# Inverse row sums of an attention repeated by a product with ones from PSUM instead of a copy

## The chip, the cores and the metric

The kernel runs on one core of one Trainium2 chip. The metric is the device time of one execution in microseconds, as the median of three timed runs. Engines are called by the profile's names: PE is TensorE's matrix unit (PEld its weight loads), DVE is VectorE, ACT ScalarE, POOL GpSimd, SP the engine that issues the DMAs.

## What is computed

Rotary attention over 2 batches, 8 heads, 576 positions and head size 64, followed by two feed-forward blocks of 512 to 2048 to 512, the first with ELU, the second with Mish:

```python
q_rot, k_rot = rotate(q), rotate(k)
scores = scale * np.matmul(q_rot, k_rot.transpose(0, 1, 3, 2))
attn = np.exp(scores - np.max(scores, axis=-1, keepdims=True))
attn = attn / (np.sum(attn, axis=-1, keepdims=True) + 1e-09)
x = np.matmul(attn, v)                     # then heads side by side: 1152 x 512
x = elu(x @ w_in) @ w_out
x = mish(x @ w2_in) @ w2_out
```

Queries, keys, values and the output are fp32, the four weights float64. Weights and activations are split into a high and a low part so that the products keep fp32's accuracy.

## The kernel before

Two heads make a pair; there are 8 pairs. The 2 x 576 query rows of a pair are cut into nine tiles of 128 rows: four full tiles of each head, and a ninth that holds the last 64 rows of both. Attention runs in windows of two tiles. The order of every engine's instructions is written out by hand in the loop over the windows, and each engine works through its own queue in that order.

In a window the names are these. `do_S` (L425, PE) makes the scores of two tiles in two PSUM tiles `ps_s`. `do_max` (L434, DVE) takes the minimum of each score row (the queries carry a minus sign), `mn`; `do_exp` (L447, ACT) writes the exponentials `P` and their row sums `sm`. In the next window `do_T` (L494, PE) transposes `P` into the PSUM tile `psT`, and `do_evac` moves `psT` into `pt`: the first tile's on DVE (L510), the second's on ACT (L512). There is one `psT`, so PE's transposes of the second tile wait for L510. `do_av` (L518, PE) adds up the product of the values `v_t` with `pt` in the PSUM tile `psA[g]`, where g is 0 for the pair's first four tiles (256 columns) and 1 for the other five (320 columns). [...]

The sums stand one to a query row, but in `psA` the queries are columns. So the inverse sums are turned around, once for each pair and g, 16 times in all. `do_eps` (L457, ACT) gathers the sums in `rc`; `repeat_inverse` (DVE) inverts them (L461) and repeats each over 64 columns into the SBUF tile `R`: 256 columns for the four full tiles (L463), and for g = 1 another 128 for the ninth tile (L469). `do_R` (L479, PE) transposes `R` into `psA[g]`, `take_R` (L484, L486, ACT) copies that back into `R`, and after the value product `do_x` (L534, DVE) multiplies `psA[g]` by it. `do_xh` (L538, ACT) and `do_xl` (L542, DVE) split the result into `XH` and `XL`.

POOL rotates queries and keys of the next pair (L293, L295, L297) and splits them (L328, L329); it also begins and ends the weights' conversion (L96, L128), whose middle steps L100, L104 and L108 are on DVE. The weights come as float64 words and are converted on the chip. After attention, `g1_mm` (L207) and `g2_first` or `g2_second` (L752, L781) are the feed-forward products on PE. `keep_warm` (L563) fills PE's first idle time with products of zeros into `psA[1]`, columns 0 to 128.

Of the kernel before, what the change touches and what calls it, by code (L numbers as in the profile page):

```python
# [14 lines left out]
ALU = mybir.AluOpType  # L15
# [7 lines left out]
def plain(ap):  # L23
    return ap.bitcast(F32)
# [3 lines left out]
def kernel(  # L28
# [11 lines left out]
    nc = tc.nc  # L40
# [213 lines left out]
    def attention(att, ps, tail):  # L254
# [2 lines left out]
        psT = ps.tile([128, 2, 512], F32, name="psT")  # L257
        psA = [ps.tile([128, 512], F32, name=f"psA{g}") for g in range(2)]
        HEAD = [(2, slice(0, HS)), (0, slice(0, 128)), (2, slice(HS, S)), (0, slice(128, HS)), (0, slice(HS, S))]
        WARM = 20  # L260
        FIRST = {(0, 0): 6, (0, 1): 2}
        FILL = (4, 5, 0)
# [6 lines left out]
        def load_pair(p):  # L269
            t = att.tile([128, 4, S], F32, tag="qk", name="qk_t", bufs=2)  # L270
            if p == 0:
                for i, cs in HEAD:
                    if i == 2:
# [25 lines left out]
        def rope_half(p, i, eng, cs=slice(0, S)):  # L299
            for k in range(3):  # L300
                rope_part(p, i, k, eng, cs)

        def split_alloc(p):
            d = {}
            for nm in ("kh", "kl") if p < MASKED else ("kh", "kl", "ql"):
                d[nm] = att.tile([128, S], F32R, tag=nm, name=nm, bufs=2)
            for nm in ("qa",) if p < MASKED else ("ka", "qa"):
                d[nm] = att.tile([128, 2, S], F32R, tag=nm, name=nm, bufs=2)
            if p >= MASKED:
                d["qh"] = att.tile([128, S], F32R, tag="qh", name="qh", bufs=1)  # L310
            i = p % 2
            d["qb"] = qb[i]
            d["bh"], d["bl"] = bd[i]
            sp_t[p] = d
            if p < MASKED:

                eng = nc.gpsimd if p else nc.vector
                for nm in ("qa", "qb"):
                    for h in range(2):
                        eng.memset(plain(d[nm][64 - 64 * h:128 - 64 * h, h, :]), 0.0)  # L320
# [13 lines left out]
        def first_hi(i, cs, heads=(0, 1)):  # L334
            x = qk_t[0][:, i, cs]
            if i:
                nc.scalar.activation(out=sp_t[0]["kh"][:, cs], in_=x, func=AF.Copy)
            for h in () if i else heads:
                nc.scalar.activation(
                    out=own(sp_t[0]["qa"], h, cs), in_=x[64 * h:64 * h + 64], func=AF.Copy, scale=QSCALE,  # L340
                )

        def first_lo(i, cs, heads=(0, 1)):
            d = sp_t[0]
            x = qk_t[0][:, i, cs]
            if i:
                nc.vector.tensor_tensor(out=d["kl"][:, cs], in0=x, in1=plain(d["kh"][:, cs]), op=ALU.subtract)
            for h in () if i else heads:
                nc.vector.scalar_tensor_tensor(
                    out=own(d["qb"], h, cs), in0=x[64 * h:64 * h + 64], scalar=QSCALE,  # L350
                    in1=plain(own(d["qa"], h, cs)), op0=ALU.mult, op1=ALU.subtract,
                )
# [22 lines left out]
        def stack_q(p):  # L375
            d = sp_t[p]
            if p >= MASKED:
                for r in range(2):
                    spread(d["qa"], d["qh"], r)
                spread(d["qb"], d["ql"], 0)  # L380
            for r in range(2):
                sl = slice(64 * r, 64 * r + 64)
                ec = slice(S - 64, S)
                hi, lo = (own(d[nm], r, ec) for nm in ("qa", "qb")) if p < MASKED else (d["qh"][sl, ec], d["ql"][sl, ec])
                nc.sync.dma_start(out=plain(d["bh"][sl, 64 * r:64 * r + 64]), in_=plain(hi))
                nc.sync.dma_start(out=plain(d["bl"][sl, 64 * r:64 * r + 64]), in_=plain(lo))
# [72 lines left out]
        def repeat_inverse(p, g):  # L459
            r = rc_t.pop((p, g))[:, :4 + g]  # L460
            nc.vector.reciprocal(out=r, in_=r)  # L461
            B = R_t[p, g] = att.tile([128, (256, 384)[g]], F32, tag=f"R{g}", name=f"R{g}", bufs=1)
            nc.vector.tensor_scalar(  # L463
                out=B[:, 0:256].rearrange("p (t h r) -> p t h r", t=2, h=2),
                in0=r[:, 0:4].rearrange("p (h t) -> p t h", h=2).unsqueeze(3).to_broadcast([128, 2, 2, 64]),
                scalar1=1.0, scalar2=0.0, op0=ALU.mult, op1=ALU.add,
            )
            if g:
                nc.vector.tensor_scalar(  # L469
                    out=B[:, 256:384], in0=r[:, 4:5].to_broadcast([128, 128]),  # L470
                    scalar1=1.0, scalar2=0.0, op0=ALU.mult, op1=ALU.add,
                )

        def do_R(p, g):
# [75 lines left out]
        for i in range(2):  # L550
            pair = []
            for nm in ("bh", "bl"):
                t = att.tile([128, 128], F32R, name=f"{nm}{i}")
# [2 lines left out]
            bd.append(pair)  # L556
        qb = [att.tile([128, 2, S], F32R, name=f"qb{i}") for i in range(2)]
        nc.vector.memset(psT[:, 1, 0:128], 0.0)
        split_alloc(0)
        split_alloc(1)  # L560
        def keep_warm(n):
            for _ in range(n):
                nc.tensor.matmul(psA[1][:, 0:128], lhsT=zero, rhs=zero, start=True, stop=True)  # L563

        zero = plain(bd[1][1])
        keep_warm(WARM)
        for i, cs in HEAD:
            rope_half(0, i, nc.vector if i else nc.gpsimd, cs)
            if cs.stop < S or i:
                first_hi(i, cs, (0,))  # L570
        for i, cs in HEAD[:-1]:
            first_lo(i, cs, (0,))
# [44 lines left out]
        for w in range(max(av_at) + 2):  # L617
# [3 lines left out]
            for u in (a, b):  # L621
                p, i = divmod(u, TPP)
# [10 lines left out]
            if R is not None:  # L633
                repeat_inverse(*R)
# [30 lines left out]
            if w == 0:  # L665
                first_hi(*HEAD[-1])
            elif w == 1:
                first_lo(*HEAD[-1])
                stack_q(0)
# [223 lines left out]
    with tc.tile_pool(name="att", bufs=1, reuse_waits="tile") as att, tc.tile_pool(  # L893
        name="ps_att", bufs=1, space=bass.MemoryType.PSUM, reuse_waits="tile"
    ) as ps:
        with tc.manual_schedule():
            attention(att, ps, tail)
# [56 lines left out]
```

## Time and profile before

| | us |
|---|---|
| timed runs: median (lowest to highest of 3) | 587.66 (587.22 to 588.53) |
| the profiled execution's own time | 589.5 |
| its span, first to last instruction | 587.7 |
| PE busy | 558.7 (95%) |
| DVE busy | 431.3 (73%) |
| ACT busy | 363.3 (62%) |
| POOL busy | 244.5 (42%) |

Busy shares are means over stages with different limits, so the rows below are read by stage. PE's granted clock is at its upper level (0.999 of full speed) over the whole span. Times in the rows count from the start of the span. A row of the timeline gives start, duration, engine, line, operation, tiles and shapes, and in brackets how long the engine stood idle before it and what ended the wait.

### The profile page before, as it was taken

To read this page: it belongs to the slowest core of one execution; us is meant where nothing else is said; L and a number is where in the kernel's file an instruction comes from. 1 tells how busy PE (TensorE), PEld (TensorE's weight loads), DVE (VectorE), ACT (ScalarE), POOL (GpSimd) and SP (SyncE) were. 2 spreads that over 40 slices of the span, in tenths; PEclk is the share of its full clock that TensorE was granted. 3 is DMA by queue.
4 is the path that set the end of the run, shared out by engine and by line. 5 is a ranking of instruction groups with operands and counts; after the bars stand their busy time and mean duration, and the time that the engine had idled before them with its cause. 6 is when DMAs were issued, how large, how long until landed. Compare 5 with 4: busy or idle time off the path is not lost.

```text
span 587.7 us, 10232 instructions
## 1 busy us (share of the span) xinstructions
PE 558.7 (95%) x3866; PEld 504.2 (86%) x3866; DVE 431.3 (73%) x650; ACT 363.3 (62%) x646; POOL 244.5 (42%) x214
## 2 busy tenths in 40 slices
PE   7879988998998999999999999999999999999997
PEld 7756756676787999999999999998989898899985
DVE  6687998888855866777778988687578687584452
ACT  3655666666665655554455564795967867668650
POOL 6768998772021233223225442253244253341000
PEclk9999999999999999999999999999999999999999
DMA  6257677636011232222223332142052332300022
GB/s 223 86 187 237 175 212 205 203 105 163 21 53 37 73 102 78 72 95 86 73 78 127 119 108 80 65 150 84 9 151 56 108 113 67 108 19 1 19 90 89
DMA packets 43121, 60.69 MB, mean 103 GB/s; under 512 B 13760, under 2 KB 31936, under 8 KB 42304
## 3 DMA queue, kind: packets, MB, share of 16 engines
q1 hardware_dynamic: 43072, 60.05, 33.8%
q8 instruction: 30, 0.49, 0.4%
q14 instruction: 19, 0.16, 0.1%
HBM read 46.20 MB, written 2.36 MB: 83 GB/s over the span
## 4 chain that ended last, share of the span: by engine, by line
PE 40%; issue 30%; DVE 15%; POOL 11%; ACT 3%; DMA 1%; SPq 0%; POOLq 0%; DVEq 0%; ACTq 0%
PE ps_h L781 17%; PE ps_s L207 14%; DVE mn L434 5%; POOL wu L96 4%; DVE pt L510 3%; PE ps_s L425 3%; PE psT L494 3%; POOL wi1l L128 2%; POOL wo0l L128 2%; DVE R L463 2%; POOL wi0l L128 2%; POOL wo1l L128 2%; ACT P L447 1%; PE psA L518 1%; DMA qk_t<-in_qk_dram 1%
## 5 line engine op out<-in xcount | busy, mean ns | idle before, releaser
L447 ACT ACTIVATE P<-ps_s,mn 128x576 f32<-128x576 f32 x72 | 52.9, 738 | 32.3 <-DVE mn L434 31.9
L494 PE MATMUL psT<-idn,P 128*128 128x128 f32 (+1 forms) x360 | 53.0, 278 | 16.8 <-DVE pt L510 16.6
L494 PEld LDWEIGHTS psT<-idn,P 128*128 128x128 f32 (+1 forms) x360 | 38.2, 134 | 33.4 <-DVE pt L510 30.4
L434 DVE TENSOR_REDUCE mn<-ps_s 128x1 f32<-128x576 f32 x72 | 51.9, 751 | 19.6 <-PE ps_s L425 19.1
L128 POOL TENSOR_TENSOR wo0l<-wu,wo0h 128x512 fp32r<-128x512 f32 x16 | 27.3, 1708 | 89.5 <-ACT wo0h L125 89.5
L100 DVE TENSOR_SCALAR wu<-wu 128x512 int32<-128x512 int32 x64 | 32.9, 513 | 35.5 <-POOL wu L96 35.5
L207 PE MATMUL ps_s<-XH,wi0h 128*128 128x288 f32 x256 | 55.1, 297 | 1.9 <-DVE tb L242 1.9
L207 PE MATMUL ps_s<-XH,wi1h 128*128 128x288 f32 x256 | 55.0, 296 | 1.5 <-ACT tb L709 1.5
L207 PE MATMUL ps_s<-XH,wi1l 128*128 128x288 f32 x256 | 54.9, 295 | 0.0
L207 PE MATMUL ps_s<-XL,wi1h 128*128 128x288 f32 x256 | 54.8, 295 | 0.0
L207 PE MATMUL ps_s<-XL,wi0h 128*128 128x288 f32 x256 | 54.6, 295 | 0.0
L207 PE MATMUL ps_s<-XH,wi0l 128*128 128x288 f32 x256 | 54.6, 295 | 0.0
L96 POOL TENSOR_SCALAR wu<-raw 128x512 f32<-128x512 f32 x64 | 48.6, 762 | 11.1 <-DMA raw<-in_w_in_dram 6.5
L104 DVE SCALAR_TENSOR_TENSOR wu<-raw,wu 128x512 int32<-128x512 int32 x64 | 49.3, 771 | 1.9
L128 POOL TENSOR_TENSOR wi1l<-wu,wi1h 128x512 fp32r<-128x512 f32 x16 | 23.0, 1441 | 66.7 <-ACT wi1h L125 66.7
L128 POOL TENSOR_TENSOR wo1l<-wu,wo1h 128x512 fp32r<-128x512 f32 x16 | 24.5, 1531 | 61.1 <-ACT wo1h L125 61.1
L108 DVE SCALAR_TENSOR_TENSOR wu<-raw,wu 128x512 int32<-128x512 int32 x64 | 48.3, 755 | 1.6
L518 PE MATMUL psA<-pt,v_t 128*64 128x256 f32 (+1 forms) x320 | 46.5, 417 | 0.0
L238 ACT ACTIVATE tb<-ps_s 128x576 f32<-128x576 f32 x30 | 19.6, 652 | 40.5 <-PE ps_s L207 38.9
L207 PEld LDWEIGHTS ps_s<-XH,wi0h 128*128 128x128 f32 x256 | 41.4, 188 | 3.6 <-DVE tb L242 2.4
L207 PEld LDWEIGHTS ps_s<-XH,wi1h 128*128 128x128 f32 x256 | 41.7, 188 | 2.3 <-ACT tb L709 1.7
L128 POOL TENSOR_TENSOR wi0l<-wu,wi0h 128x512 fp32r<-128x512 f32 x16 | 23.0, 1442 | 47.1 <-ACT wi0h L125 47.1
(150 smaller groups left out, 1522.2 us busy)
## 6 DMA issues: line engine op xcount, KB each, us to landing
raw<-in_w_in_dram SPq DMA_DIRECT2D x32, 512.0 KB, 3.7
raw<-in_w_out_dram SPq DMA_DIRECT2D x32, 512.0 KB, 3.3
qk_t<-in_qk_dram SPq DMA_DIRECT2D x6, 1152.0 KB, 5.3
qa<-qh SPq DMA_DIRECT2D x24, 144.0 KB, 2.5
v_t<-in_vp_dram SPq DMA_DIRECT2D x8, 320.0 KB, 3.0
out_dram<-Y SPq DMA_DIRECT2D x9, 256.0 KB, 2.0
ka<-kh SPq DMA_DIRECT2D x12, 144.0 KB, 2.8
ka<-kl SPq DMA_DIRECT2D x12, 144.0 KB, 2.5
```

The costliest lines, as they stand in the source:

```text
L96: nc.gpsimd.tensor_scalar(out=u, in0=high.bitcast(F32), scalar1=REBASE, scalar2=0.0, op0=ALU.mult, op1=ALU.add)
L100: nc.vector.tensor_scalar(out=ui, in0=ui, scalar1=3, scalar2=0x7FFFFFF8, op0=ALU.logical_shift_left, op1=ALU.bitwise_and)
L104: nc.vector.scalar_tensor_tensor(out=ui, in0=high, scalar=-0x80000000, in1=ui, op0=ALU.bitwise_and, op1=ALU.bitwise_or)
L108: nc.vector.scalar_tensor_tensor(out=ui, in0=low, scalar=29, in1=ui, op0=ALU.logical_shift_right, op1=ALU.bitwise_or)
L128: nc.gpsimd.tensor_tensor(out=lo, in0=u, in1=plain(hi), op=ALU.subtract)
L207: nc.tensor.matmul(o[:, j, :HS], lhsT=w[:, cc, :], rhs=x[:, b, cc, j * HS:j * HS + HS], start=(k == 0), stop=(k == 3 * NC - 1),)
L238: nc.scalar.activation(out=v2(g), in_=h, func=AF.Relu, scale=-1.0)
L434: nc.vector.tensor_reduce(out=m, in_=psS[u][:, :, :HS], axis=AX.XY, op=ALU.min)
L447: nc.scalar.activation(out=P.rearrange("p (j n) -> p j n", j=2), in_=psS.pop(u)[:, :, :HS], func=AF.Exp, scale=-1.0, bias=mn_t.pop(u), acc ...
L494: nc.tensor.transpose(tv[:w, c, :], P[:, c * 128:c * 128 + w], idn)
L518: nc.tensor.matmul(o[64 * h:64 * h + 64, :n], lhsT=v_t[p][:, c, 64 * h:64 * h + 64], rhs=pt_t[p, g][:, h, c, :], start=(c == 0), stop=(c = ...
L781: nc.tensor.matmul(o, lhsT=l, rhs=w, start=(k == 0), stop=(k == 3 * GF - 1))
```

## The change

Both copies in `repeat_inverse` become products. The first operand is a stretch of ones in `psA[g]`, columns 384 to 512, which no product or transpose writes; the second is the inverse sums, repeated by the access pattern as before. The ones are written once, by two memsets on DVE at the start.

```diff
+        ONES = slice(384, 512)
...
             B = R_t[p, g] = att.tile([128, (256, 384)[g]], F32, tag=f"R{g}", name=f"R{g}", bufs=1)
-            nc.vector.tensor_scalar(
+
+            ones = psA[g][:, ONES]
+            nc.vector.tensor_tensor(
                 out=B[:, 0:256].rearrange("p (t h r) -> p t h r", t=2, h=2),
-                in0=r[:, 0:4].rearrange("p (h t) -> p t h", h=2).unsqueeze(3).to_broadcast([128, 2, 2, 64]),
-                scalar1=1.0, scalar2=0.0, op0=ALU.mult, op1=ALU.add,
+                in0=ones.rearrange("p (h r) -> p h r", h=2).unsqueeze(1).to_broadcast([128, 2, 2, 64]),
+                in1=r[:, 0:4].rearrange("p (h t) -> p t h", h=2).unsqueeze(3).to_broadcast([128, 2, 2, 64]),
+                op=ALU.mult,
             )
             if g:
-                nc.vector.tensor_scalar(
-                    out=B[:, 256:384], in0=r[:, 4:5].to_broadcast([128, 128]),
-                    scalar1=1.0, scalar2=0.0, op0=ALU.mult, op1=ALU.add,
+                nc.vector.tensor_tensor(
+                    out=B[:, 256:384], in0=ones, in1=r[:, 4:5].to_broadcast([128, 128]), op=ALU.mult
                 )
...
         nc.vector.memset(psT[:, 1, 0:128], 0.0)
+        for g in range(2):
+            nc.vector.memset(psA[g][:, ONES], 1.0)
```

The order of every engine stays the same. On DVE, at the first pair's g = 1, the queue held before (`mn` row minima, `rc` sums, `R` their repeated inverses, `pt` the emptied transposes):

```order
L510 COPY pt_331<-psT 128x5x128
L461 RECIPROCAL rc<-rc 128x5
L463 TENSOR_SCALAR R_436<-rc 128x256
L469 TENSOR_SCALAR R_436<-rc 128x128
L434 TENSOR_REDUCE mn<-ps_s 128x1 x2
```

and at the same place in the changed kernel, whose lines are numbered a little higher:

```order
L513 COPY pt_333<-psT 128x5x128
L462 RECIPROCAL rc<-rc 128x5
L466 TENSOR_TENSOR R_438<-psA_79,rc 128x256
L473 TENSOR_TENSOR R_438<-psA_79,rc 128x128
L435 TENSOR_REDUCE mn<-ps_s 128x1 x2
```

Only the two instructions that write `R` differ; they now read `psA` as well. The waits on semaphores are the same too.

## Rows read from the trace of the kernel before

**Rows 1.** Busy time by stretch: from:to, length, engines' busy us (instructions), clock, DMA

```profile
21.00:170.00 149.00, 132.08 (x1000) 101.21 (x999) 122.77 (x195) 96.06 (x232) 99.66 (x79) 1.00 0.56 162
170.00:588.00 418.00, 410.44 (x2760) 387.84 (x2758) 294.56 (x428) 258.48 (x396) 131.09 (x114) 1.00 0.26 79
```

**Rows 2.** Waits of PE, 35.9 to 136 us: total, times, longest

```profile
PE psT L494 <- DVE pt L510: 12.0, 13, 1.7
```

**Rows 3.** Group of line L463: count, busy us, mean ns, idle before

```profile
L463 DVE TENSOR_SCALAR R<-rc 128x256 f32<-128x256 f32 x16 | 11.6, 723 | 0.5
```

**Rows 4.** Single lines of DVE: shortest, median, longest in ns; first and last start

```profile
L463 DVE TENSOR_SCALAR R<-rc x16: 293/644/1486, 21.2 to 167.9; 128x256 f32<-128x256 f32 x16
L469 DVE TENSOR_SCALAR R<-rc x8: 214/689/697, 37.3 to 168.1; 128x128 f32<-128x128 f32 x8
L542 DVE TENSOR_TENSOR XL<-psA,XH x16: 410/450/493, 44.9 to 184.5; 128x256 fp32r<-128x256 f32 x8, 128x320 fp32r<-128x320 f32 x8
```

**Rows 5.** Timeline of POOL and DVE, 84 to 88 us

```profile
84.16 1.89 POOL L295 TENSOR_TENSOR qk_t<-qk_t,tab 128x576 f32<-128x576 f32 x1
84.69 0.41 DVE L542 TENSOR_TENSOR XL<-psA,XH 128x256 fp32r<-128x256 f32 x1
85.02 0.16 DVE L461 RECIPROCAL rc<-rc 128x4 f32<-128x4 f32 x1
85.22 0.99 DVE L463 TENSOR_SCALAR R<-rc 128x256 f32<-128x256 f32 x1
```

**Rows 6.** Timeline of the first pair's g = 1, 35.8 to 41 us

```profile
35.81 1.43 POOL L297 TENSOR_TENSOR qk_t<-qk_t 128x576 f32<-128x576 f32 x1
35.90 1.49 DVE L463 TENSOR_SCALAR R<-rc 128x256 f32<-128x256 f32 x1
37.20 0.72 POOL L328 TENSOR_SCALAR kh<-qk_t 128x576 fp32r<-128x576 f32 x1
37.28 0.43 PE L425 MATMUL ps_s<-kl,qa 128*128 128x288 f32 x2
37.31 0.70 DVE L469 TENSOR_SCALAR R<-rc 128x128 f32<-128x128 f32 x1
37.91 1.41 DVE L434 TENSOR_REDUCE mn<-ps_s 128x1 f32<-128x576 f32 x2
39.25 0.81 DVE L510 COPY pt<-psT 128x640 f32<-128x640 f32 x1
40.11 0.77 PE L494 MATMUL psT<-idn,P 128*128 128x128 f32 x5 [1.28 <-DVE pt L510]
```

**Rows 7.** Timeline of PE, 104 to 106 us

```profile
104.37 1.30 PE L518 MATMUL psA<-pt,v_t 128*64 128x320 f32 x8
```

**Rows 8.** Timeline of DVE, 151 to 154 us, where POOL is idle

```profile
151.83 0.29 DVE L463 TENSOR_SCALAR R<-rc 128x256 f32<-128x256 f32 x1
152.04 0.22 DVE L469 TENSOR_SCALAR R<-rc 128x128 f32<-128x128 f32 x1
152.49 1.42 DVE L434 TENSOR_REDUCE mn<-ps_s 128x1 f32<-128x576 f32 x2 [0.23 <-PE ps_s L425]
```

**Rows 9.** Timeline of DVE and PE, 131 to 136 us

```profile
131.53 1.39 DVE L463 TENSOR_SCALAR R<-rc 128x256 f32<-128x256 f32 x1
133.44 1.41 DVE L434 TENSOR_REDUCE mn<-ps_s 128x1 f32<-128x576 f32 x2
135.64 0.76 PE L494 MATMUL psT<-idn,P 128*128 128x128 f32 x5 [1.74 <-DVE pt L510]
```

**Rows 10.** Timeline of DVE at the start

```profile
5.17 0.46 DVE L293 TENSOR_TENSOR qk_t<-qk_t,tab 128x288 f32<-128x288 f32 x1 [0.75 <-DMA qk_t<-in_qk_dram]
```

**Rows 11.** Groups of DVE, 44 to 160 us, and line L104's shortest, median, longest

```profile
L104 DVE SCALAR_TENSOR_TENSOR wu<-raw,wu 128x512 int32<-128x512 int32 x7 | 6.6, 946 | 0.0
L108 DVE SCALAR_TENSOR_TENSOR wu<-raw,wu 128x512 int32<-128x512 int32 x6 | 6.3, 1048 | 0.0
L104 DVE SCALAR_TENSOR_TENSOR wu<-raw,wu x64: 676/693/1672, 59.3 to 526.5; 128x512 int32<-128x512 int32 x64
```

## The prediction

> **What bounds the kernel now.** I first read the busy times by stage, to find the engine that a saved microsecond must reach. From 170 us to the end TensorE works 410.44 of 418 us: the two feed-forward stages are TensorE's, and nothing that the change touches runs there except at their very start. In the attention stage, 21 to 170 us, TensorE works 132.08 of 149 us, VectorE 122.77, GpSimd 99.66 [rows 1]. So attention has 17 us in which TensorE stands still, and VectorE is the nearest to full. The view of waits then says who TensorE waits for: between 35.9 and 136 us it waited 13 times, 12.0 us in all, and each time for the VectorE line that empties psT, L510 [rows 2]. What counts is therefore whether VectorE reaches L510 earlier in those windows.
>
> Next come the instructions that the change replaces. The 16 copies of L463 take 11.6 us, 723 ns each on average [rows 3]. That mean hides two kinds: L463 runs from 293 to 1486 ns for the same 256 columns, L469 from 214 to 697 ns. The nearest thing to the new instruction, L542 (one operand in psA, one in SBUF, result in SBUF), stays between 410 ns (256 columns) and 493 ns (320) [rows 4]. Why L463 stretches is seen where both run under one GpSimd instruction. L295 on GpSimd lasts from 84.16 to 86.05. L542 starts at 84.69 inside it and takes 0.41 us, its bare time. L463 starts at 85.22 inside it and ends at 86.21, just after GpSimd ends [rows 5]. The first pair shows the same twice: L463 and L469 end at 37.39 and 38.01, after GpSimd ends at 37.24 and 37.92 [rows 6]. Where GpSimd is idle the pair takes 0.29 and 0.22 us [rows 8]. I went through all 24 copies: each long one ends 0.1 to 0.2 us after a GpSimd instruction ends, each short one has no GpSimd work beside it. So a copy from SBUF alone waits until GpSimd is through; an instruction with one operand in PSUM does not.
>
> **What the change costs and saves.** The product reads ones from psA and the sums from SBUF, writes SBUF, and is queued exactly where the copy was, behind the same single wait. A product of 256 columns should take L542's 0.41 us; 64 more columns cost L542 about 0.08 us, so 128 columns take some 0.27 us. From start to next start it is less, since VectorE's instructions overlap: L542 at 84.69 is followed after 0.33 us by the next instruction (the reciprocal). I take 0.33 us for 256 columns, and 0.20 for 128 (0.33 less twice 0.067). A product for g=0 then occupies 0.33 us of the queue, the two for g=1 0.53. The bounds for this unseen form: from below the bare copy, 0.26 and 0.21 us; from above L542's full duration with no overlap, 0.41 and 0.27. Over the ten places below (four of 256 columns, six pairs) the ends move the sum by 0.5 us up or 0.9 us down, since at 35.90 and 102.76 something else sets the gain.
>
> Ten of the sixteen places have a GpSimd instruction beside them. For each I take the gap from the start of L463 to the start of the next row-minimum L434. After the change the gap is 0.33 or 0.53, unless the scores that L434 reads come later. L434 is followed by L510, so what the gap loses L510 gains, and TensorE's following transpose L494 gains it up to the length of its wait:
> - 35.90: gap 2.01, the scores set it. The second score product ends at 37.71, the second minimum starts at 37.74, and L510 0.67 us later at 38.41 instead of 39.25. Gain 0.84, of a TensorE wait of 1.28 [rows 6].
> - 55.14: 0.95 to 0.53, gain 0.42 of 1.31. 64.08: 0.69 to 0.33, gain 0.36 of 0.50. 76.07: 1.04 to 0.53, gain 0.51 of 1.73. 85.22: 0.91 to 0.33, gain 0.58 of 1.01. 93.56: 1.91 to 0.53, gain 1.38 of 1.73.
> - 102.76: 0.79 to 0.33, but TensorE is busy with the value product until 105.67 and begins its transpose 0.08 us later [rows 7]: gain 0.05.
> - 114.02: 1.05 to 0.53, the scores hold it by another 0.12: gain 0.40 of 0.98. 123.17: 0.91 to 0.33, gain 0.58 of 1.00.
> - 131.53: 1.91 to 0.53, gain 1.38 of 1.74, the last of the ten [rows 9].
>
> The sum is 6.5 us. Every gain fits into its wait, so TensorE moves by it, and everything behind TensorE too.
>
> The other six places have bare copies, which grow by about 0.07 us (256 columns) or 0.1 us (pair). At 21.21, 45.39, 140.74 and 151.83 the minimum behind them waits for the scores anyway, at 151.83 for 0.23 us [rows 8]. At 160.17 and 167.88 TensorE is busy with other products past the point at which it needs the result. I put these at nothing; without that cover they would cost 0.5 us. The two new memsets sit at the head of VectorE's queue, among memsets of 0.17 us; behind them L293 waits 0.75 us for its load [rows 10], which covers 0.3 us. The warm-up products of TensorE wait for an earlier memset and do not move.
>
> The profiled execution took 589.5 us with a span of 587.7 us; 6.5 less is 583.0 and a span of 581.2. It lies 1.8 us above the median of the three timed runs, 587.66. The same 6.5 us off the median gives 581.2 us, 1.1% less.
>
> [...] Bare, the copy of 256 columns takes 0.29 us and an instruction with a PSUM operand 0.41 [rows 4]. [...]
>
> **Rivals.** First: the gain is taken back at the next instruction that GpSimd holds up. VectorE also makes the weights' integer passes (L100, L104, L108), all in SBUF. From 44 to 160 us the seven of L104 take 6.6 us and the six of L108 6.3, where 13 bare ones at 0.68 would take 8.8 [rows 11]: they lose 4.1 us. If such a pass comes earlier while GpSimd's instruction ends when it did, it ends when it did, and the transpose behind it too. For it: GpSimd is busy two thirds of the stage [rows 1], so a pass that comes earlier seldom finds it idle. Against: after most of these passes the next minimum waits for scores. If half of the gain goes so, 3.3 us stay: 584.4 us.
>
> Second: the passes fall better than before. How long one waits depends only on where in a GpSimd instruction it falls, from nothing (0.68 us in all) to a whole one (1.67 us, the longest L104), and shifted by 1 to 6 us they all fall anew. If four passes on the path wait some 0.5 us less each, the gain is 8.5: 579.2 us.
>
> Third, the other side: the long copies are long for a reason that the product shares, so it waits for GpSimd as well and only the rate changes. Its place is the ten gaps: ten times 0.12 and six times 0.07 more, 1.6 us: 589.3 us, slower. It decides if the product's durations spread with GpSimd's. Against it stand all 16 copies of L542, none above 493 ns.
>
> Fourth: nothing is left, because GpSimd, or the loads that follow it, sets the pace of attention once VectorE is faster: 587.7 us. Against it: from 35.9 to 136 us TensorE waited for nothing but L510 [rows 2].
>
> **How the numbers follow.** The forecast has 0.53 (580.7 to 582.1 us by the bounds of the product's cost), taken back 0.20, falls better 0.20, slower 0.04, nothing left 0.03. The time given is the forecast's, 581.2. The range goes from 578.8, a little below the second rival, to 584.6, just above the first. A measurement here tells about 0.2%, 1.2 us, from no change: forecast and the first two rivals are faster, 0.93; same 0.03; slower 0.04.
>
> **What would show it.** Right: all products of 256 columns near 0.41 us and of 128 near 0.28 whatever GpSimd does; TensorE's waits for L510 in the attention stage down from about 12 us to about 5.5; the feed-forward stages as long as before, only starting 6 to 7 us earlier. Wrong: a spread in the products' durations (third rival), unchanged gaps with longer weight passes (first), or a new wait of TensorE for a load (fourth).

## The result, and the profile after

| | before | after |
|---|---|---|
| median of 5 runs | 587.60 us (587.22 to 588.53) | 580.23 us (579.38 to 581.99) |
| ratio, 95% interval | | 0.987 [0.9855, 0.9884] |
| profiled execution | 589.5 us, span 587.7 us | 581.99 us, span 580.2 us |
| granted clock, mean | 0.999 | 0.999 |

The kernel is 7.4 us faster where 6.5 were forecast (581.2 us). The time lies half a microsecond below the forecast's own range (580.7 to 582.1 us), inside the larger one (578.8 to 584.6), and halfway between the forecast and its second rival (579.2). The lines moved: L463 is now L466, L469 is L473, L434 is L435, L510 is L513, L494 is L497.

Busy time by stretch, in the columns of [rows 1], cut where the attention stage now ends:

```profile
21.00:164.00 143.00, 132.85 (x1007) 102.02 (x1005) 115.48 (x194) 96.12 (x233) 99.60 (x80) 1.00 0.59 169
164.00:581.00 417.00, 408.95 (x2749) 386.96 (x2748) 296.06 (x428) 257.66 (x396) 127.98 (x112) 1.00 0.26 80
```

TensorE does the same work in the first stretch (132.85 us against 132.08) in 143 us instead of 149. Its idle time there has shrunk from 17 to 10 us. Feed-forward is as long as it was (417 us against 418).

The new instructions, in the columns of [rows 4]:

```profile
L466 DVE TENSOR_TENSOR R<-psA,rc x16: 424/425/425, 20.9 to 160.6; 128x256 f32<-128x256 f32 x16
L473 DVE TENSOR_TENSOR R<-psA,rc x8: 280/280/283, 36.0 to 160.9; 128x128 f32<-128x128 f32 x8
```

This is the reading that matters: the shortest and the longest of the 16 products are 1 ns apart, where the copies spread from 293 to 1486. GpSimd is as busy as before (99.60 us), so nothing about its work changed. Only VectorE's waiting for it is gone from these instructions.

TensorE's waits for the emptying of psT, from 15 to 175 us, first in the kernel before and then in the kernel after (total, times, longest):

```profile
PE psT L494 <- DVE pt L510: 16.6, 19, 1.7
```

```profile
PE psT L497 <- DVE pt L513: 9.9, 17, 1.7
```

The difference of 6.7 us is nearly the whole gain. Three places of the timeline of after, and the start of TensorE's queue:

```profile
1.95 1.44 PE L568 MATMUL psA<-bl 128*128 128x128 f32 x5 [1.95 <-DVE psA L563]
...
35.58 1.43 POOL L298 TENSOR_TENSOR qk_t<-qk_t 128x576 f32<-128x576 f32 x1
35.68 0.42 DVE L466 TENSOR_TENSOR R<-psA,rc 128x256 f32<-128x256 f32 x1
36.02 0.28 DVE L473 TENSOR_TENSOR R<-psA,rc 128x128 f32<-128x128 f32 x1
36.73 1.56 DVE L435 TENSOR_REDUCE mn<-ps_s 128x1 f32<-128x576 f32 x2 [0.43 <-PE ps_s L426]
38.20 0.82 DVE L513 COPY pt<-psT 128x640 f32<-128x640 f32 x1
39.07 0.77 PE L497 MATMUL psT<-idn,P 128*128 128x128 f32 x5 [0.45 <-DVE pt L513]
...
72.01 1.28 POOL L128 TENSOR_TENSOR wi0l<-wu,wi0h 128x512 fp32r<-128x512 f32 x1
72.03 1.80 DVE L104 SCALAR_TENSOR_TENSOR wu<-raw,wu 128x512 int32<-128x512 int32 x1
...
76.71 0.76 PE L497 MATMUL psT<-idn,P 128*128 128x128 f32 x5 [1.59 <-DVE pt L513]
...
116.07 0.72 DVE L108 SCALAR_TENSOR_TENSOR wu<-raw,wu 128x512 int32<-128x512 int32 x1
```

At the first place, both products run wholly under L298 of GpSimd (35.58 to 37.01) and are through at 36.30. The minimum then waits 0.43 us for the scores, as forecast. TensorE's wait of 1.28 us [rows 6] is now 0.45: 0.83 gained, 0.84 forecast.

### The profile page after: what moved, and what is told of

It is laid out like the page before. It is cut to its first block, busy times and chain, and to the rows that moved or that the text cites. A ratio compares the mean times of both kernels' runs of the same rounds, so it can differ in the third digit from the quotient of the medians.

```text
span 580.2 us, 10234 instructions
## 1 busy us (share of the span) xinstructions
PE 557.8 (96%) x3866; PEld 504.0 (87%) x3866; DVE 425.9 (73%) x652; ACT 362.8 (63%) x646; POOL 241.1 (42%) x214
## 4 chain that ended last, share of the span: by engine, by line
PE 45%; issue 29%; POOL 11%; DVE 10%; ACT 2%; DMA 1%; SPq 0%; POOLq 0%; DVEq 0%
PE ps_h L786 17%; PE ps_s L207 14%; PE ps_s L426 5%; PE psT L497 5%; POOL wu L96 4%; DVE mn L435 3%; PE psA L521 3%; DVE pt L513 3%; POOL wi1l L128 2%; POOL wo0l L128 2%; POOL wi0l L128 2%; POOL wo1l L128 2%; DMA qk_t<-in_qk_dram 1%; ACT P L448 1%; PE psA L482 1%
## 5 line engine op out<-in xcount | busy, mean ns | idle before, releaser
L435 DVE TENSOR_REDUCE mn<-ps_s 128x1 f32<-128x576 f32 x72 | 52.1, 753 | 19.2 <-PE ps_s L426 18.4
L497 PE MATMUL psT<-idn,P 128*128 128x128 f32 (+1 forms) x360 | 53.1, 278 | 9.9 <-DVE pt L513 9.9
L128 POOL TENSOR_TENSOR wo0l<-wu,wo0h 128x512 fp32r<-128x512 f32 x16 | 25.4, 1590 | 88.4 <-ACT wo0h L125 79.0
L497 PEld LDWEIGHTS psT<-idn,P 128*128 128x128 f32 (+1 forms) x360 | 38.2, 135 | 26.3 <-DVE pt L513 23.3
L100 DVE TENSOR_SCALAR wu<-wu 128x512 int32<-128x512 int32 x64 | 31.9, 498 | 33.4 <-POOL wu L96 33.4
L96 POOL TENSOR_SCALAR wu<-raw 128x512 f32<-128x512 f32 x64 | 48.6, 761 | 11.5 <-DMA raw<-in_w_in_dram 6.9
L104 DVE SCALAR_TENSOR_TENSOR wu<-raw,wu 128x512 int32<-128x512 int32 x64 | 49.9, 779 | 1.9
L108 DVE SCALAR_TENSOR_TENSOR wu<-raw,wu 128x512 int32<-128x512 int32 x64 | 48.2, 752 | 1.6
L207 PEld LDWEIGHTS ps_s<-XH,wi1l 128*128 128x128 f32 x256 | 41.3, 188 | 0.0
```

The costliest lines, as they stand in the source:

```text
L96: nc.gpsimd.tensor_scalar(out=u, in0=high.bitcast(F32), scalar1=REBASE, scalar2=0.0, op0=ALU.mult, op1=ALU.add)
L100: nc.vector.tensor_scalar(out=ui, in0=ui, scalar1=3, scalar2=0x7FFFFFF8, op0=ALU.logical_shift_left, op1=ALU.bitwise_and)
L104: nc.vector.scalar_tensor_tensor(out=ui, in0=high, scalar=-0x80000000, in1=ui, op0=ALU.bitwise_and, op1=ALU.bitwise_or)
L108: nc.vector.scalar_tensor_tensor(out=ui, in0=low, scalar=29, in1=ui, op0=ALU.logical_shift_right, op1=ALU.bitwise_or)
L128: nc.gpsimd.tensor_tensor(out=lo, in0=u, in1=plain(hi), op=ALU.subtract)
L207: nc.tensor.matmul(o[:, j, :HS], lhsT=w[:, cc, :], rhs=x[:, b, cc, j * HS:j * HS + HS], start=(k == 0), stop=(k == 3 * NC - 1),)
```

## The experiments

Two theories stood against each other from the start. Mine: one operand in PSUM is what lets the instruction run beside GpSimd, and the gain is what the copies lost. The rival: the gain has another source (the operation tensor_tensor instead of tensor_scalar, the memsets, or weight passes that fall anew). The second question was where the 0.9 us beyond the forecast came from.

### 1. The same product with the ones in SBUF

```diff
-            ones = psA[g][:, ONES]
+            ones = one_t
...
-        for g in range(2):
-            nc.vector.memset(psA[g][:, ONES], 1.0)
+        one_t = att.tile([128, 128], F32, name="one_t")
+        nc.vector.memset(one_t, 1.0)
```

> The product stays, but its ones lie in SBUF (128 columns, written once) and not in psA. [...] Then the products stretch again at the ten places with GpSimd beside them, to about 0.5 to 1.6 us from about 0.42 bare, and the time is 587 to 590 us, the copy's or a little more because the bare product is 0.12 us longer. [...]

Measured: 592.27 us, 1.0072 [1.0056, 1.0087] of before. Single lines:

```profile
L466 DVE TENSOR_TENSOR R<-one_t,rc x16: 425/774/1610, 20.5 to 171.1; 128x256 f32<-128x256 f32 x16
L473 DVE TENSOR_TENSOR R<-one_t,rc x8: 284/746/1494, 36.9 to 171.5; 128x128 f32<-128x128 f32 x8
```

The same operation with the same shapes spreads again, from its bare 425 ns to 1610. So it is not the operation. The rate is the product's and the waiting is the copy's, which makes this the third rival of the prediction come true: it gave 589.3 us, 587 to 590 us were expected here, and the run shows more. Part of the reason is seen in one place:

```profile
53.32 1.60 POOL L296 TENSOR_TENSOR qk_t<-qk_t,tab 128x576 f32<-128x576 f32 x1
54.32 0.89 DVE L466 TENSOR_TENSOR R<-one_t,rc 128x256 f32<-128x256 f32 x1
55.01 1.47 POOL L298 TENSOR_TENSOR qk_t<-qk_t 128x576 f32<-128x576 f32 x1
55.13 1.49 DVE L473 TENSOR_TENSOR R<-one_t,rc 128x128 f32<-128x128 f32 x1
56.55 1.41 DVE L435 TENSOR_REDUCE mn<-ps_s 128x1 f32<-128x576 f32 x2
57.88 0.81 DVE L513 COPY pt<-psT 128x640 f32<-128x640 f32 x1
58.74 1.21 PE L497 MATMUL psT<-idn,P 128*128 128x128 f32 x5 [2.05 <-DVE pt L513]
```

L466 ends at 55.21, past the end of L296 and just after L298 has started. L473 then starts inside L298 and waits it out as well. TensorE stood idle for 2.05 us, and what followed is its granted clock (the number before the last two):

```profile
58.00:60.00 2.00, 1.26 (x7) 1.22 (x8) 1.79 (x4) 0.89 (x5) 1.92 (x3) 0.73 0.54 127
60.00:62.00 2.00, 2.00 (x10) 2.00 (x9) 0.86 (x2) 1.28 (x3) 2.00 (x2) 0.50 0.73 175
62.00:64.00 2.00, 2.00 (x16) 1.38 (x16) 1.82 (x4) 1.51 (x4) 2.00 (x2) 0.92 0.89 206
```

The granted clock is down to 0.50 for some 3.4 us; two score products together take 0.66 to 0.83 us there, and 0.42 to 0.51 from 65 us on. Another such stretch follows an idle time of 1.93 us at 99 us (0.68 to 0.82 us for two). This I had not counted; the two stretches account for the 3 us beyond the rival's price, if each is worth the 1.5 us that experiment 4 finds for one. One of the four executions shows a mean granted clock of 0.997 where the other three show 0.994, and it is the shortest, 590.95 us.

A long wait did not always bring the clock down. A third one in this trace is as long as the second, and the clock behind it stays at 1.00:

```profile
138.81 0.77 PE L497 MATMUL psT<-idn,P 128*128 128x128 f32 x5 [1.93 <-DVE pt L513]
```

```profile
140.00:142.00 2.00, 2.00 (x17) 1.58 (x17) 1.53 (x3) 1.60 (x6) 0.00 (x0) 1.00 0.99 228
```

What else decides, no run here shows.

### 2. The copy kept, but reading its sums from PSUM

```diff
-            nc.vector.reciprocal(out=r, in_=r)
+            q = psA[g][:, 384:388 + g]
+            nc.vector.reciprocal(out=q, in_=r)
+            r = q
```

There are no ones and no product; the reciprocal writes five columns of psA, and the two tensor_scalar copies read them.

> The copy stays as before, but the reciprocal writes its 4 or 5 columns into psA (columns 384 on) and the copies read them there; no ones, no memsets. Theory (one operand in PSUM is enough): the copies take about 0.40 to 0.43 us for 256 columns and 0.28 for 128 whatever GpSimd does, and the time is that of the change, 580.2 us within 0.7. Rival (the operation counts, a copy waits and a product does not): spread from 0.4 to 1.5 us as before and 587 us.

Measured: 581.76 us, 0.9893 [0.9879, 0.9908]. The copies:

```profile
L465 DVE TENSOR_SCALAR R<-psA x16: 424/425/425, 20.5 to 160.3; 128x256 f32<-128x256 f32 x16
L471 DVE TENSOR_SCALAR R<-psA x8: 280/281/283, 35.5 to 160.7; 128x128 f32<-128x128 f32 x8
```

The copy with its input in PSUM has the product's durations within a nanosecond. Its time misses the expected 580.2 us within 0.7: it is 1.5 us above, though the intervals of the two ratios still overlap. The traces differ by 0.1 us only (counted from the first place on, the lead over before grows by 7.0 us here and by 7.1 in after); where the rest comes from is not shown. Together with experiment 1 this settles what frees these instructions: for copy and product alike, it is the operand in PSUM and not the operation.

It does not follow that every instruction from SBUF waits. The reciprocal just ahead reads and writes SBUF alone, and it is never held up, under L295 of GpSimd in [rows 5] for instance (0.16 us):

```profile
L461 DVE RECIPROCAL rc<-rc x16: 160/176/191, 21.0 to 167.7; 128x4 f32<-128x4 f32 x8, 128x5 f32<-128x5 f32 x8
```

Side by side: 425 ns flat with one operand in PSUM, 425 to 1610 with both operands in SBUF (experiment 1), 293 to 1486 for the tensor_scalar from SBUF [rows 4], 160 to 191 for the reciprocal from SBUF. What spares the reciprocal, whether that it is short or something else, this run does not show.

### 3. The memsets alone

```diff
         nc.vector.memset(psT[:, 1, 0:128], 0.0)
+        for g in range(2):
+            nc.vector.memset(psA[g][:, 384:512], 1.0)
```

> The copies of before, with the two memsets of the change at the head, whose ones nobody reads. Theory: the memsets lie under the wait for the first load and the warm-up products start 0.5 us later without a price, so time as before, 587.7 us within 0.5. Rival: a part of the 7.4 us comes from the later head, because the weight passes fall anew against GpSimd; then 585 us or less with the same long copies.

Measured: 587.75 us, 0.9999 [0.999, 1.0008]. The memsets cost and bring nothing. As in after, the first warm-up product starts at 1.96 us instead of 1.48, since it now waits for them.

### 4. The two halves apart

The product for g = 1 alone (256 and 128 columns), then for g = 0 alone (256 columns); the other half keeps the copy:

```diff
+            if g == 1:
+                ones = psA[g][:, ONES]
+                nc.vector.tensor_tensor(
...
+            else:
                 nc.vector.tensor_scalar(
```

> Only the places with g = 1 (the pairs of instructions) use the product, g = 0 keeps the copy. By the sum over places: 0.84 + 0.42 + 0.51 + 1.38 + 0.40 + 1.38 = 4.9 us less than before: 582.7 us. Rival (a shift of any size makes the weights' integer passes fall anew, and that moves as much as the places themselves): off from that by 1 us or more, and the two halves do not add up to 7.4 us.

> Only the places with g = 0 use the product. By the sum over places: 0.36 + 0.58 + 0.05 + 0.58 = 1.6 us less than before: 586.0 us; with the other half 6.5 us together. Rival (the integer passes fall anew): off by 1 us or more, with durations of L100, L104 and L108 that differ from before by as much.

Measured: g = 1 alone 580.96 us, 0.9883 [0.9868, 0.9898]; g = 0 alone 587.4 us, 0.9993 [0.9981, 1.0005]. The gains, 7.0 and 0.6 us, add up to 7.6, near the change's 7.4, but the split is not that of the places: 4.9 and 1.6 were expected. In the trace of g = 0 alone, most of what its own places bring is lost at one point. There a pair of copies (g = 1) starts at 74.87 and the emptying of psT behind it at 77.27; TensorE stands idle, then runs slowly, and the next emptying has lost another 0.83 us against before:

```profile
78.13 0.77 PE L508 MATMUL psT<-idn,P 128*128 128x128 f32 x5 [2.11 <-DVE pt L524]
```

```profile
76.00:78.00 2.00, 0.02 (x2) 0.00 (x0) 2.00 (x4) 1.28 (x3) 1.97 (x2) 1.00 0.80 188
78.00:80.00 2.00, 1.87 (x14) 1.87 (x15) 0.55 (x3) 1.30 (x5) 2.00 (x2) 0.89 0.99 230
80.00:82.00 2.00, 2.00 (x11) 1.60 (x11) 1.42 (x3) 1.43 (x4) 1.92 (x3) 0.50 0.72 162
82.00:84.00 2.00, 2.00 (x12) 0.77 (x10) 1.98 (x4) 0.82 (x4) 2.00 (x2) 0.76 0.09 17
```

In the trace of before the transpose at this place waited 1.73 us, and the granted clock stayed at 1.00 in the 6 us behind it. So a few tenths of a microsecond more of idle time had a second price here, if the clock is the cause.

The trace is one of ten executions of this kernel. Five show a mean clock of 0.996 or 0.997 over the span, as this one does, and took 587.56 to 589.63 us; the other five show 1.00 and took 586.42 to 587.24. Their medians are 588.17 and 586.64 us. So the drop came in half of the executions of one and the same kernel, and cost about 1.5 us where it came. Without it g = 0 alone gains 1.3 us, near the 1.6 expected; it is then the 7.0 of g = 1 that lies off.

### 5. TensorE kept at work in that wait

Six products into unused columns, ahead of the waiting transpose, in the kernel with the product for g = 0 alone:

```diff
+            if w == 14:
+                for _ in range(6):
+                    nc.tensor.matmul(psT[:, 1, 256:384], lhsT=idn, rhs=idn, start=True, stop=True)
             if 0 < w <= NW:
                 do_T(b - 2)
```

> The product for the halves with g=0 alone (587.4 us), with six extra products of TensorE into unused columns just ahead of the transpose that there waited 2.11 us, after which the granted clock was 0.50 for about 3.4 us. Theory: the stretch at the lower clock follows from that long idle time; with the six products (0.85 us) in it the transpose waits about 1.2 us, the granted clock stays at 1.00, and the step of +0.83 us at the next emptying of psT goes: 586.4 us. Rival: the step is VectorE's own, and stays with the clock at 1.00: 587.4 us.

Measured: 588.62 us, 1.0015 [1.0004, 1.0025] of before. It tests nothing: the columns are unused, but they belong to psT, so the products waited for its emptying as the transpose had.

```profile
78.04 2.61 PE L671 MATMUL psT<-idn 128*128 128x128 f32 x12 [2.09 <-DVE pt L524]
```

(The six products are recorded as twelve.) The idle time was as long, the clock fell again (0.50 from 79 to 81 us; five of the eleven executions show a mean clock of 0.997), and the products came on top. The second try puts them into `psA[1][:, 0:128]`, free at this point; nothing else differs.

> As in the first try, the product for g=0 alone with six extra products of TensorE ahead of the transpose that waits 2.1 us at 76 to 78 us; they now go to columns of psA1 that are free there, so that they don't wait for psT themselves. Theory: TensorE works 0.85 us of that idle time, the granted clock stays at 1.00, and the step of +0.83 us at the next emptying of psT goes: 586.4 us against 587.4 for the product with g=0 alone. Rival: the step is VectorE's own and stays with the clock at 1.00: 587.4 us.

Measured: 586.16 us, 0.9973 [0.9963, 0.9984].

```profile
74.89 1.60 PE L671 MATMUL psA<-idn 128*128 128x128 f32 x12
77.06 0.76 PE L508 MATMUL psT<-idn,P 128*128 128x128 f32 x5 [0.56 <-DVE pt L524]
```

```profile
77.00:79.00 2.00, 1.95 (x16) 1.95 (x17) 0.63 (x2) 1.31 (x5) 2.00 (x2) 1.00 1.01 232
79.00:81.00 2.00, 2.00 (x17) 1.26 (x17) 2.00 (x4) 1.63 (x6) 1.92 (x3) 1.00 0.71 164
81.00:83.00 2.00, 2.00 (x17) 1.55 (x13) 1.97 (x4) 1.14 (x4) 2.00 (x2) 1.00 0.12 22
```

The products took 1.60 us, not 0.85, and filled most of the wait. VectorE works as late as before at this point, yet the clock stays at 1.00, and the next emptying of psT comes 0.84 us earlier against the one before it. So the drop of the clock is the cause of that step in the trace, and the filled wait keeps it away: none of the nine executions shows it (mean clock 0.999 or 1.00). The median falls by 1.2 us (1.0 was expected), but it mixes two cases: against the executions of experiment 4 with the drop the filled kernel is 2.0 us faster, against those without it 0.5.

### 6. The weights' passes cut to one column

Before and after, each with this edit (n is 1 for the jobs of the attention stage and 512 otherwise, in all three passes), so that the passes L100, L104 and L108 nearly vanish there:

```diff
+            n = 1 if pause else 512
             nc.vector.tensor_scalar(
-                out=ui, in0=ui, scalar1=3, scalar2=0x7FFFFFF8, op0=ALU.logical_shift_left, op1=ALU.bitwise_and
+                out=ui[:, :n], in0=ui[:, :n], scalar1=3, scalar2=0x7FFFFFF8, op0=ALU.logical_shift_left, op1=ALU.bitwise_and
             )
...
```

> Before, with the integer passes of the eight weight jobs of the attention stage over one column in place of 512, so that most of these weights stay unconverted; VectorE loses some 17 us of work between 40 and 160 us, 4 to 5 of it waits for GpSimd. Read together with the same edit of the changed kernel. Theory: the change's own places are worth about 6.5 us and the rest of its 7.4 us comes from passes that fall better, so without passes the two kernels differ by 6 to 6.8 us. Rival: the whole 7.4 us lies at the places, and the difference stays at 7.4 or more.

> After, with the integer passes of the eight weight jobs of the attention stage over one column in place of 512, so that most of these weights stay unconverted. Theory: 6 to 6.8 us below the same edit of the kernel before, all of it at places where a long copy stood. Rival: 7.4 us or more.

Measured: 583.71 us (0.993 [0.9918, 0.9943]) and 578.25 us (0.9837 [0.9823, 0.985]). They differ by 5.5 us: less than either expectation. TensorE's waits from 15 to 175 us, in the shortened before and then in the shortened after:

```profile
PE psT L495 <- DVE pt L511: 12.2, 15, 1.7
```

```profile
PE psT L498 <- DVE pt L514: 7.5, 13, 1.7
```

They shrink by 4.7 us. By the starts of the emptyings the lead grows at six of the ten places only, by 4.9 us in all, and changes by under 0.2 us anywhere else. The other four gain 0.03 us at most: there a copy meets less of GpSimd, the scores hold the minimum, or TensorE has no wait. So the expectation was wrong in taking the places for fixed. A copy's loss depends on when it comes, and cutting the passes moved the copies. The edit also left the passes some waiting (L109, the third pass, took 488 ns on average for its one column). The difference can't be read as "places without passes"; what holds is that gains appear only where TensorE waits behind a copy.

The shortened passes also separate what experiment 2 leaves open. In the shortened before, the first pass, a tensor_scalar over one column from SBUF, takes 0.14 us inside an instruction of GpSimd; the third, over one column as well but with two SBUF inputs, waits until GpSimd is through:

```profile
67.08 1.41 POOL L298 TENSOR_TENSOR qk_t<-qk_t 128x576 f32<-128x576 f32 x1
67.47 0.14 DVE L101 TENSOR_SCALAR wu<-wu 128x1 int32<-128x1 int32 x1
...
95.97 1.41 POOL L294 TENSOR_TENSOR qk_t<-qk_t,tab 128x576 f32<-128x576 f32 x1
96.21 1.19 DVE L109 SCALAR_TENSOR_TENSOR wu<-raw,wu 128x1 int32<-128x1 int32 x1
```

Over 512 columns the tensor_scalar L100 does wait (412 to 1502 ns in after). So of the instructions that read SBUF alone, some wait for GpSimd and some do not, and a short one is not spared for being short.

### 7. Two ways further

**The passes in PSUM.** If one operand in PSUM is enough, the integer passes should be freed too. Six jobs lead theirs through unused columns of psT (384) and psA (128), two instructions a pass:

```diff
+            parts = scratch or [(ui, slice(0, 512))]
+            for t, cs in parts:
+                nc.vector.tensor_scalar(
+                    out=t, in0=ui[:, cs], scalar1=3, scalar2=0x7FFFFFF8,
+                    op0=ALU.logical_shift_left, op1=ALU.bitwise_and,
+                )
...
```

> After, with the three integer passes of six weight jobs in the attention stage led through unused PSUM columns (384 and 128 columns a pass). Theory, one operand in PSUM is enough to pass GpSimd by: pieces of about 0.55 and 0.28 us whatever GpSimd does, where the passes now take 0.73, 1.02 and 0.93 us on average; VectorE loses about 4.6 us of work between 40 and 155 us, half of it reaches TensorE's waits: 578 us. Rival, integer work or the strided operand is held up anyway: pieces with a spread, and two instructions for one: 582 us.

Measured: 604.99 us, 1.0302 [1.0281, 1.0323]. The first pass, shortest, median and longest, and a wait of VectorE from 35 to 170 us:

```profile
L102 DVE TENSOR_SCALAR psT<-wu x6: 560/560/562, 53.2 to 158.9; 128x384 int32<-128x384 int32 x6
L102 DVE TENSOR_SCALAR psA<-wu x6: 282/282/284, 53.6 to 159.4; 128x128 int32<-128x128 int32 x6
```

```profile
DVE psT L102 <- ACT pt L525: 11.0, 6, 2.0
```

The pieces are as flat as forecast, for integers and for an output in PSUM too. The time went elsewhere: a pass that writes into psT waits until ScalarE has emptied it (11.0 us in six times, and 17.4 more for the other two passes), although its columns are its own, and everything behind it on VectorE waits too. The same trap as in experiment 5, where the products waited 2.09 us: neither wait went by the columns. In both cases the columns lie in the same tile as the transposes; whether it is the tile that decides is not shown.

**The sums repeated by ScalarE**, from SBUF, in place of the product:

```diff
-            nc.vector.tensor_tensor(
+            nc.scalar.activation(
                 out=B[:, 0:256].rearrange("p (t h r) -> p t h r", t=2, h=2),
-                in0=ones.rearrange("p (h r) -> p h r", h=2).unsqueeze(1).to_broadcast([128, 2, 2, 64]),
-                in1=r[:, 0:4].rearrange("p (h t) -> p t h", h=2).unsqueeze(3).to_broadcast([128, 2, 2, 64]),
-                op=ALU.mult,
+                in_=r[:, 0:4].rearrange("p (h t) -> p t h", h=2).unsqueeze(3).to_broadcast([128, 2, 2, 64]),
+                func=AF.Copy,
```

> After, with the sums repeated by ScalarE from SBUF in place of VectorE's product. Theory, VectorE's 0.33 or 0.53 us a place sit on the path where the scores don't set the next minimum: TensorE's waits for the emptying of psT drop from 7 to about 5 us, 578.5 us. Rival, ScalarE's copies (about 0.4 and 0.7 us a place) stand ahead of the exponentials and delay them and the transposes behind: 582 us or more.

Measured: 578.91 us, 0.985 [0.9836, 0.9863]. In its trace the attention stage ends 3.1 us earlier than in after's (0.6 of it stood before the first place), and TensorE's waits for psT are down from 9.9 us to

```profile
PE psT L493 <- DVE pt L509: 7.6, 16, 1.7
```

It is the fastest kernel measured here with the whole computation in it. Against after alone the measurement does not quite separate the two (the intervals of the ratios overlap by 0.0008). The traces differ by 2.4 us at and behind the places, but they are one execution each, and after's is the longest of its five (581.99 us).

## Why the prediction was right

**What bounds.** Right: the gain lies in attention, in TensorE's waits for the emptying of psT. From 35.9 us on, in after's time to 130 us, 5.3 us of them are left of the 12.0 [rows 2]; about 5.5 was forecast.

**The product's cost.** Right: 0.425 and 0.280 us whatever GpSimd does, against 0.41 and 0.27 put in. The next product starts 0.34 us after the first (35.68 to 36.02), 0.33 put in; behind one of 128 columns the minimum starts after 0.20 us (54.25 to 54.45), 0.20 put in. What spoke against the change, the longer bare time, shows as well: 128 more columns cost the bare copy 79 ns (214 to 293) and the product 145 (280 to 425), and a bare product is 0.13 us longer. In the ten places the wait that went was longer than that.

One reading of the copies was wrong, without a price. A short copy can have GpSimd beside it, if it has started first:

```profile
55.96 0.21 DVE L469 TENSOR_SCALAR R<-rc 128x128 f32<-128x128 f32 x1
55.97 1.47 POOL L297 TENSOR_TENSOR qk_t<-qk_t 128x576 f32<-128x576 f32 x1
```

Too wide was also "a copy from SBUF alone waits": the wait is not a matter of SBUF by itself (experiments 2 and 6).

**The ten places.** The gain at a place is how much earlier the emptying of psT behind it starts in after than in before, beyond the lead it had at the emptying before:

| copy at (before) | forecast, us | measured, us |
|---|---|---|
| 35.90 | 0.84 | 0.83 |
| 55.14 | 0.42 | 0.61 |
| 64.08 | 0.36 | 0.33 |
| 76.07 | 0.51 | 0.14 |
| 85.22 | 0.58 | 0.45 |
| 93.56 | 1.38 | 1.36 |
| 102.76 | 0.05 | 0.15 |
| 114.02 | 0.40 | 0.40 |
| 123.17 | 0.58 | 1.07 |
| 131.53 | 1.38 | 1.38 |
| sum | 6.50 | 6.72 |

Five agree within 0.03 us. Two large misses lie in the weights' passes ahead of the place, which fell anew. In before, the L104 ahead of 76.07 and the L108 ahead of 123.17 took

```profile
74.49 1.44 DVE L104 SCALAR_TENSOR_TENSOR wu<-raw,wu 128x512 int32<-128x512 int32 x1
...
121.00 1.72 DVE L108 SCALAR_TENSOR_TENSOR wu<-raw,wu 128x512 int32<-128x512 int32 x1
```

and in after 1.80 and 0.72 (above): the first took 0.36 us of the gain back, the second gave 1.00 us, of which 0.49 reached the place. Two smaller ones have the same cause: ahead of 55.14 L100 took 1.31 us in place of 1.50, ahead of 85.22 L108 took 1.85 in place of 1.72. The miss at 102.76 (0.10 us) I have not followed up. Two emptyings away from the ten places gain 0.48 us more, 0.39 of it behind an L104 of 1.03 us in place of 1.44. Places and these two make 7.2 us; the median says 7.4. (Another 0.22 us of lead stood before the first place in this pair of traces.) That the sum came so near is in part luck: the misses are 0.78 us up and 0.56 down.

**First and second rival.** Both work at once: of the passes in the stage, some take back and some give, and over the stage giving won by about 0.7 us (0.22 at the places and 0.48 besides). The forecast counted neither, and this is its mis-sized term: its own range covered the product's cost alone, so the measured time fell out of it. L104 as a group got longer (7 of them 7.2 us from 40 to 155 us) and L108 shorter (6, 5.6 us) than in [rows 11]; L100 got shorter too (7, 5.1 us in place of 6.0). That the passes fall anew is shown by the trace of g = 1 alone: behind the place at 123.17, whose copy it keeps, the emptying comes 1.01 us earlier, since L108 ahead of it takes 0.71 us in place of 1.72. A part of it changes with the execution and not with the kernel: in the trace of the memsets alone, which keeps every copy, two emptyings move by 0.20 and 0.17 us against before.

**Third rival.** Excluded for this kernel, and seen at work in experiment 1, with a larger price than forecast (592.3 us against 589.3). Behind two waits there, of 1.93 and 2.05 us, TensorE's clock came down, which it did behind no wait in before (1.00 in every 2 us from 4 to 172 us); that this is the whole difference is an estimate.

**The bare places and the memsets.** Next to nothing, as forecast: from 135 to 171 us, past the last bare places, the lead goes from 7.37 to 7.29 us, and the memsets alone time as before (experiment 3). One step was wrong without a price: the warm-up products do wait for the new memsets (1.95 us in place of 1.48), since these write psA, which the warm-up writes too. The first score product comes no later (7.94 us, 7.97 before).

**Fourth rival.** Excluded: the lead of 7.3 us at the end of the attention stage is one of 7.5 us at the end of the span (587.7 to 580.2), 0.2 of both from before the first place.

## What to carry to other kernels

Where VectorE and GpSimd work side by side, look at the shortest and the longest time of each VectorE line: here the line whose copies spread by a factor of five waited for GpSimd, and moving one operand into PSUM made it flat (424 to 425 ns), even though its bare time grew (0.29 to 0.425 us). Count the gain place by place, as the smaller of what the instruction loses and what the bounding engine waits behind it, and expect the other instructions that wait for GpSimd to fall anew, in both directions; here single passes changed by up to 1.00 us. Columns that lay unused in someone else's tile were not free: in experiments 5 and 7 the waits did not go by columns (2.09 us, and 11.0 us in six waits), so put scratch where the tile's owner is idle.

## What the runs showed of the hardware that was not expected

- TensorE's clock fell behind single waits within the stage. Behind idle times of 2.05 us (experiment 1), 2.11 us (experiment 4) and 2.09 us (experiment 5, first try) the granted clock went from 1.00 to 0.50 for about 3.4 us, and behind one of 1.93 us in experiment 1 two score products took 0.68 to 0.82 us as well, while behind the 1.7 us waits of before and after it stayed at 1.00, as it did behind another wait of 1.93 us in experiment 1. By the mean clocks of its ten executions the kernel of experiment 4 had the drop in five, at about 1.5 us each; with the wait filled none of nine had it. So a longer wait had a second price here that a count of idle time doesn't show, and that came in some executions only.
- The waiting between VectorE and GpSimd went both ways. In before, L96 of GpSimd takes 1.08 us at 75.36 and 1.10 at 113.30, where it starts while L104 of VectorE is at work (74.49 to 75.93 and 113.18 to 113.88), and 0.64 to 0.71 at its other seven places up to 171 us.
- An integer instruction of VectorE from SBUF into PSUM (560 to 562 ns for 384 columns) was as untouched by GpSimd as the float ones (424 to 425 ns for 256).
- ScalarE repeated the sums from SBUF in 406 to 415 ns (256 columns, 16 times), whatever GpSimd did.
